# A DiT block on one core: reordering the transposes, scale matmuls and modulations of the first four chunks of the K projection

## The chip, the cores and the metric

The kernel runs on one core of one Trainium2 chip. The metric is device time in microseconds (us), median over executions. A profile is the trace of a single execution; its span (first to last instruction) is about 1.8 us shorter than the device time of the same execution. The kernels ran in four series, each with runs of before in it, and times are compared within a series: the second of the table of results ran on chip 3, the third on chip 9, another with experiments alone on chip 15. A load "lands" when all its data have arrived. Engines are named TensorE (PE), VectorE (DVE), ScalarE (ACT), GpSimd (POOL). "PEld" is TensorE's weight load.

## The reference

```python
mod = (_silu(c) @ w_mod).reshape(B, 6, 1, D)          # B, N, D = 2, 256, 1152
shift_a, scale_a, gate_a, shift_m, scale_m, gate_m = [mod[:, i] for i in range(6)]
h = _layernorm(x) * (1 + scale_a) + shift_a
qkv = (h @ wqkv)...                                    # then attention, wo, residual
... h2 = _layernorm(x) * (1 + scale_m) + shift_m; m = _gelu(h2 @ w_fc1) @ w_fc2
```

Only the beginning matters: normalise x, multiply by (1 + scale_a), multiply by the K part of wqkv. The kernel adds the shift later.

## The kernel before

x has 512 rows: four tiles of 128 (tiles 0 and 1 are batch 0, tiles 2 and 3 are batch 1). D = 1152 is nine chunks of 128. To feed TensorE, each tile is normalised by VectorE (`norm1`, which needs the tile's `rstd`, the reciprocal of its standard deviation), transposed chunk by chunk on TensorE into PSUM (`transpose_x`; PSUM is the memory that the kernel's matmuls and transposes write to, in parts called banks), and multiplied by the scale while it is copied out of PSUM (`modulate`). The scales themselves come from TensorE (`scale_group`) and from weights that are still being loaded. `k_step(k, ...)` does the K matmuls of chunk k for six of the nine output panels of 128 columns; the other three ("wide panels", L311 in the traces) follow when all chunks are done. The parts that the change touches:

```python
def scale_group(k0, k1, tile_of=aux_tile):
    pm = tile_of([P, k1 - k0, B], "pm")
    for j in range(k0, k1):
        ...                                   # 9 matmuls with 2 columns for each chunk j
            nc.tensor.matmul(pm[:, j - k0, :], w_scale_a[:, k, j * P:(j + 1) * P], sT[:, k, 0:B], ...)
def modulate(pt, i, k, b, j0, eng):
    dst, src, sc = hT0[:, k, b * N:(b + 1) * N], pt[:, i, j0:j0 + N], scale_a[:, k, b:b + 1]
    ...                                       # VectorE if eng == "d", else ScalarE
def both(pt, k):
    for b, e in enumerate("da"):
        modulate(pt, 0, k, b, b * N, e)
...
norm1(1, 0, CUT); norm1(0, 0, CUT)            # CUT = 4 chunks = 512 columns
pt_a = transpose_x([0, 1], BT[0])             # chunks 0-1 of tiles 0 and 1
... root_exp(2, 3)                            # ScalarE: rstd of tile 2, the last one
norm1(3, 0, CUT)
pm0, pm1 = [scale_group(k, k + 1, acc_tile) for k in range(2)]
nc.vector.tensor_scalar_mul(hT0[:, 0, 0:N], pt_a[:, 0, :], pm0[:, 0, 0:1])
... modulate(pt_a, 1, 1, 0, 0, "d")
norm1(2, 0, CUT)
transpose_x([0, 1], [3], pt_c, 1)
fill(1)                                       # one filler matmul of 512 columns
k_step(0, 0, N); k_step(1, 0, N, 0, 2)        # batch 0
transpose_x([0, 1], [2], pt_c, 0)             # needs tile 2's norm
k_step(1, 0, N, 2)
modulate(pt_c, 0, 0, 1, 0, "d"); modulate(pt_c, 1, 1, 1, 0, "a")
...
k_step(0, N, T)                               # batch 1
pm = scale_group(2, 4)
pt_b = transpose_x([2, 3], BT[0])
... k_step(1, N, T)
pt_d = transpose_x([2, 3], BT[1])
... k_step(2, 0, N); k_step(2, N, T)
for k in range(3, KD):
    split = 2 if k == 5 else 0
    k_step(k, 0, T, 0, split)
    if k in (3, 5, 7): scale_add(scale_group(k + 1, k1), ...)
    if k < KD - 1: both(transpose_x([k + 1], range(NT)), k + 1)
    k_step(k, 0, T, split)
```

## Time and profile before

| | us |
|---|---|
| device time before the prediction, median of 3 runs | 243.68 (243.38 to 243.81) |
| span of the profiled execution (its device time: 243.17) | 241.4 |
| TensorE busy | 236.6 (98%) |
| K projection: first transpose to first wide panel matmul (start 8.48, end 25.38) | 16.89 |

From the page of before: busy time of the engines, then the chain of work that ended last, by engine.

```profile
PE 236.6 (98%) x1698; PEld 144.9 (60%) x1698; DVE 91.5 (38%) x193; ACT 59.9 (25%) x121; POOL 28.3 (12%) x47
...
PE 94%; issue 2%; ACT 2%; POOL 1%; DVE 0%; POOLq 0%; DVEq 0%; ACTq 0%
```

TensorE bounds the kernel. A change at the start can only shorten the time by removing TensorE's breaks there. The timeline of TensorE in before, 8.4 to 14 us (columns: start us, us, engine, line, operation, output<-inputs, shapes, count; consecutive instructions of one group are merged):

```profile
8.48 0.40 PE L266 MATMUL pt<-ident,xn 128*128 128x128 bf16 x4 [0.23 <-DVE xn L235]
8.81 0.17 PE L247 MATMUL pm<-ones_row 1*128 1x2 bf16 x1
8.91 0.60 PE L249 MATMUL pm<-sT,w_scale_a 128*128 128x2 bf16 x18
9.38 0.27 PE L266 MATMUL pt<-ident,xn 128*128 128x128 bf16 x2
9.49 0.38 PE L325 MATMUL pwarm<-zeros 128*128 128x512 bf16 x1
9.74 1.03 PE L282 MATMUL pk<-big,w_k 128*128 128x256 bf16 x8
11.07 0.28 PE L266 MATMUL pt<-ident,xn 128*128 128x128 bf16 x2 [0.30 <-DVE xn L235]
11.19 1.42 PE L282 MATMUL pk<-big,w_k 128*128 128x256 bf16 x10
12.45 0.59 PE L249 MATMUL pm<-sT,w_scale_a 128*128 128x2 bf16 x18
12.91 0.38 PE L266 MATMUL pt<-ident,xn 128*128 128x128 bf16 x4
13.13 0.82 PE L282 MATMUL pk<-big,w_k 128*128 128x256 bf16 x6
13.78 0.39 PE L266 MATMUL pt<-ident,xn 128*128 128x128 bf16 x4
```

How to read it: the second column runs to the end of the last matmul's result, which lies some 0.2 us behind its issue; so count starts, not ends. Unmerged, a K matmul of 256 columns starts every 0.109 us and a transpose every 0.056 us. A bracket gives the engine's idle time before the instruction and what ended it; for TensorE it counts from the end of the last result, and is so some 0.16 us less than what the stream of issues lost. Eight K matmuls from 9.74 on are issued by 10.61, yet the next transposes start at 11.07: 0.46 us of waiting. Inside the ten matmuls from 11.19 on, the fifth starts 0.28 us after the fourth instead of 0.11: a second wait of 0.17. What they wait for, from the timelines of ScalarE and VectorE in before:

```profile
10.31 0.20 ACT L340 ACTIVATE rstd<-rstd 128x1 f32<-128x1 f32 x1
...
10.60 0.41 DVE L235 TENSOR_SCALAR xn<-x_sb,mv,rstd 128x512 bf16<-128x512 bf16 x1 [0.40 <-ACT rstd L340]
11.40 0.35 DVE L272 TENSOR_SCALAR big<-pt,scale_a 128x256 bf16<-128x256 bf16 x1 [0.38 <-PE pt L266]
```

ScalarE's rstd of tile 2 ends at 10.51, VectorE's norm of tile 2 runs 10.60 to 11.01, the transposes follow, then VectorE's modulation of chunk 0, batch 1, until 11.75. That chain (rstd, norm, transpose, modulation, matmul) is the critical path of this stretch.

### The profile page before, as it was taken

The page shows a single profiled execution, that of the slowest core. Times are in us where ns is not written, and L with a number is a line of the kernel's source. Part 1 is how long each engine was busy: PE and PEld are TensorE (multiplying, and loading weights), DVE is VectorE, ACT ScalarE, POOL GpSimd, SP SyncE. Part 2 cuts the span into 40 slices and gives each one's busy share as a digit, 9 for nine tenths or more (in the row PEclk, how much of TensorE's full clock was granted, in tenths as well). Part 3 has the DMA queues.
Part 4 walks back from the last instruction along what each step waited for, and adds up shares of the span by engine and source line. Part 5 has one row for each costly group of instructions (what it writes and reads, how often), then busy time and mean ns, then how long its engine had stood idle before and what let it go on. Part 6 is the DMA issues. An engine that isn't in the chain of part 4 may idle for free.

```text
span 241.4 us, 3989 instructions
## 1 busy us (share of the span) xinstructions
PE 236.6 (98%) x1698; PEld 144.9 (60%) x1698; DVE 91.5 (38%) x193; ACT 59.9 (25%) x121; POOL 28.3 (12%) x47
## 2 busy tenths in 40 slices
PE   8999999999999999999999999999999999999994
PEld 5675444476667666888844444444666666566674
DVE  4842442319325678830002999950000000000001
ACT  6723322307215032771423333222000000000000
POOL 2300000002300324100000000001121111111111
PEclk9999999999999999999999999999999999999999
DMA  6999999996599997739999999999200000000000
GB/s 221 323 316 322 376 368 393 388 392 214 120 332 397 388 272 77 196 61 366 390 391 391 339 326 282 278 327 281 98 16 16 20 16 16 19 18 17 26 25 16
DMA packets 48925, 53.30 MB, mean 221 GB/s; under 512 B 9731, under 2 KB 36619, under 8 KB 48907
## 3 DMA queue, kind: packets, MB, share of 16 engines
q1 hardware_dynamic: 41312, 50.14, 62.4%
q10 hardware_dynamic: 7083, 1.72, 5.3%
q0 software_dynamic: 512, 1.19, 1.8%
q8 instruction: 13, 0.21, 0.4%
q14 instruction: 5, 0.04, 0.1%
HBM read 50.15 MB, written 1.19 MB: 213 GB/s over the span
## 4 chain that ended last, share of the span: by engine, by line
PE 94%; issue 2%; ACT 2%; POOL 1%; DVE 0%; POOLq 0%; DVEq 0%; ACTq 0%
PE pacc L748 29%; PE pacc L804 29%; PE pacc L695 7%; PE pacc L601 7%; PE pq L523 7%; PE pk L282 5%; PE pk L311 2%; PE pa L642 2%; PE ps_s L558 2%; PE pn L418 2%; ACT sink L208 1%; PE pt L266 1%; PE pm L249 1%; PE pg L500 0%; ACT rstd L337 0%
## 5 line engine op out<-in xcount | busy, mean ns | idle before, releaser
L748 PE MATMUL pacc<-hT,w_f 128*128 128x256 bf16 (+1 forms) x432 | 70.5, 326 | 0.0
L804 PE MATMUL pacc<-w_f,gT 128*128 128x384 bf16 (+2 forms) x468 | 70.5, 314 | 0.0
L804 PEld LDWEIGHTS <-gT 128*128 128x128 bf16 x468 | 44.4, 98 | 26.2
L748 PEld LDWEIGHTS <-w_f 128*128 128x128 bf16 x432 | 42.2, 98 | 27.6
L810 DVE TENSOR_TENSOR tmp<-pacc,gate 128x384 f32<-128x384 f32 (+2 forms) x13 | 6.9, 527 | 65.6 <-PE pacc L804 57.4
L780 ACT ACTIVATE gT<-pacc 128x512 bf16<-128x512 f32 x24 | 14.3, 597 | 32.7 <-PE pacc L748 32.7
L471 DVE SCALAR_TENSOR_TENSOR part<-w_gate_m,s,part 128x1152 f32<-128x1152 bf16 x16 | 21.3, 1409 | 0.0
L812 POOL TENSOR_TENSOR o_sb<-tmp,x 128x384 bf16<-128x384 f32 (+1 forms) x12 | 11.7, 972 | 54.0 <-DVE tmp L810 54.0
L695 PE MATMUL pacc<-w_o,big 128*128 128x384 bf16 x108 | 17.9, 326 | 0.0
L523 PE MATMUL pq<-hT,w_q 128*128 128x512 bf16 x81 | 17.8, 379 | 0.0
L601 PE MATMUL pacc<-w_v,hT 128*128 128x384 bf16 x108 | 17.7, 326 | 0.0
L601 PEld LDWEIGHTS <-hT 128*128 128x128 bf16 x108 | 10.5, 98 | 7.1 <-issue 0.3
L695 PEld LDWEIGHTS <-big 128*128 128x128 bf16 x108 | 10.4, 98 | 7.2 <-issue 0.4
L523 PEld LDWEIGHTS <-w_q 128*128 128x128 bf16 x81 | 7.9, 98 | 9.4
L282 PE MATMUL pk<-big,w_k 128*128 128x256 bf16 (+1 forms) x72 | 13.3, 326 | 0.0
L701 POOL TENSOR_TENSOR x<-tmp,x_sb 128x384 f32<-128x384 f32 x8 | 7.3, 912 | 26.8 <-DMA w_scale_m<-in_w_mod_dram 14.9
L469 DVE TENSOR_SCALAR part<-w_gate_m,s 128x1152 f32<-128x1152 bf16 x2 | 1.5, 816 | 22.1 <-DMA w_gate_m<-in_w_mod_dram 22.1
L493 POOL DMA_DIRECT2D gates_dram<-nat_v x2 | 1.1, 534 | 67.7 <-DVE nat_v L491 67.7
L282 PEld LDWEIGHTS <-w_k 128*128 128x128 bf16 x72 | 6.7, 98 | 3.7 <-issue 0.3
L769 ACT ACTIVATE gT<-pacc 128x512 bf16<-128x512 f32 x12 | 6.5, 598 | 8.8 <-PE pacc L748 8.8
L514 POOL DMA_DIRECT2D gates_dram<-nat x4 | 2.4, 602 | 49.6 <-DVE nat L511 48.7
L175 PE MATMUL pwarm<-zeros 128*128 128x256 f32 x18 | 7.0, 560 | 1.2 <-DVE eps_t L95 1.2
(102 smaller groups left out, 164.9 us busy)
## 6 DMA issues: line engine op xcount, KB each, us to landing
w_f<-in_w_fc_dram SPq DMA_DIRECT2D x12, 864.0 KB, 14.3
w_f<-in_w_fc_dram SPq DMA_DIRECT2D x3, 1728.0 KB, 10.0
w_f<-in_w_fc_dram SPq DMA_DIRECT2D x2, 2592.0 KB, 17.3
w_gate_a<-in_w_mod_dram SPq DMA_DIRECT2D x3, 864.0 KB, 12.7
w_v<-in_wqkv_dram SPq DMA_DIRECT2D x3, 864.0 KB, 13.9
w_o<-in_wo_dram SPq DMA_DIRECT2D x3, 864.0 KB, 14.0
w_shift_m<-in_w_mod_dram SPq DMA_DIRECT2D x3, 864.0 KB, 8.8
w_scale_m<-in_w_mod_dram SPq DMA_DIRECT2D x3, 864.0 KB, 15.0
```

Source lines behind the costliest of these rows:

```text
L175: nc.tensor.matmul(dst[:, 0:T // 2], zeros32[:, 0:P], zeros32, start=True, stop=True)
L282: nc.tensor.matmul(pk[m][:, c0:c1], w_k[:, k, m * P:(m + 1) * P], hT0[:, k, c0:c1], start=(k == 0 and c0 == 0), stop=(k == KD - 1), skip_g ...
L471: nc.vector.scalar_tensor_tensor(part[:, b, :], wg[:, k, :], s32[:, k, b:b + 1], part[:, b, :], op0=ALU.mult, op1=ALU.add,)
L523: nc.tensor.matmul(pq[m][:], w_q[:, k, m * P:(m + 1) * P], hT[:, k, :], start=(k == 0), stop=(k == KD - 1), skip_group_check=True,)
L601: nc.tensor.matmul(pacc[:], hT[:, k, t * P:(t + 1) * P], w_v[:, k, pnl * PW:(pnl + 1) * PW], start=(k == 0), stop=(k == KD - 1),)
L695: nc.tensor.matmul(pacc[:], aT[:, k, t * P:(t + 1) * P], w_o[:, k, c0:c1], start=(k == 0), stop=(k == KD - 1),)
L701: (nc.gpsimd if pool_add else nc.vector).tensor_tensor(x1[:, t, c0:c1], tmp[:], x_sb[:, t, c0:c1], op=ALU.add)
L748: nc.tensor.matmul(dst, w_f1[m // KD][:, k, ml * P:(ml + 1) * P], hT[:, k, c0:c1], start=start, stop=(k == KD - 1), **kw,)
L780: nc.scalar.activation(gT[:, m, :], pacc[:], ACT.Gelu_apprx_tanh)
L804: nc.tensor.matmul(pacc[:], gT[:, kk, t * P:(t + 1) * P], w_f2[j][:, r, c0 - n * PW:c0 - n * PW + cw], start=(kk == 0), stop=(kk == KF - 1),)
L810: nc.vector.tensor_tensor(tmp[:], pacc[:], gate_m[:, b, c0:c0 + cw], op=ALU.mult)
L812: (nc.vector if last else nc.gpsimd).tensor_tensor(o_sb[:], tmp[:], x1[:, t, c0:c0 + cw], op=ALU.add)
```

## The change

Its intent: transpose all four chunks of tiles 0 and 1 at once, and of tile 3 too, before tile 2 is ready; put the scales of chunks 2-3 into the part of the same bank that is no longer used; let ScalarE and VectorE share modulations; and split tile 2's norm so that its first two chunks can be transposed earlier.

```diff
-    pt_a = transpose_x([0, 1], BT[0])
+    pt_a = transpose_x([0, 1, 2, 3], BT[0])
...
-    norm1(2, 0, CUT)
-    pt_c = aux_tile([P, 2, N], "pt", BF16)
-    transpose_x([0, 1], [3], pt_c, 1)
+    norm1(2, 0, N)
+    norm1(2, N, CUT)
+    pt_c = aux_tile([P, 4, N], "pt", BF16)
+    transpose_x([0, 1, 2, 3], [3], pt_c, 1)
     fill(1)                                   # and the filler has 256 columns instead of 512
     k_step(0, 0, N)
     k_step(1, 0, N, 0, 2)
+    modulate(pt_c, 0, 0, 1, 0, "a", P, N)
     transpose_x([0, 1], [2], pt_c, 0)
     k_step(1, 0, N, 2)
-    modulate(pt_c, 0, 0, 1, 0, "d")
+    modulate(pt_c, 0, 0, 1, 0, "d", 0, P)
...
     k_step(0, N, T)
-    pm = scale_group(2, 4)
-    pt_b = transpose_x([2, 3], BT[0])
+    pm = pt_a[:, 0, 0:4 * B].bitcast(FP32).rearrange("p (j b) -> p j b", b=B)
+    scale_group(2, 4, pm=pm)
+    for i in (2, 3):
+        nc.tensor.transpose(pt_c[:, i, 0:P], xns[2][:, i * P:(i + 1) * P], ident[:])
     scale_add(pm, 2, 4)
-    modulate(pt_b, 0, 2, 0, 0, "d")
-    modulate(pt_b, 1, 3, 0, 0, "a")
+    for b, e in enumerate("da"):
+        for i in (2, 3):
+            modulate((pt_a, pt_c)[b], i, i, b, 0, e)
     norm1(2, CUT, D)
+    norm1(3, CUT, D)
     k_step(1, N, T)
-    pt_d = transpose_x([2, 3], BT[1])         # and the modulations and the norm that followed it
     k_step(2, 0, N)
     k_step(2, N, T)
     for k in range(3, KD):
-        split = 2 if k == 5 else 0
+        split = 2 if k in (3, 5) else 0
```

More of the change, by code (lines that the diff above doesn't have):

```diff
@@ L241, with scale_group @@
     scale_a = act.tile([P, KD, B], FP32, name="scale_a")
-    def scale_group(k0, k1, tile_of=aux_tile):
-        pm = tile_of([P, k1 - k0, B], "pm")
+    def scale_group(k0, k1, tile_of=aux_tile, pm=None):
+        if pm is None:
+            pm = tile_of([P, k1 - k0, B], "pm")
         for j in range(k0, k1):
@@ L267, in transpose_x, with modulate @@
         return pt
-    def modulate(pt, i, k, b, j0, eng):
-        dst, src, sc = hT0[:, k, b * N:(b + 1) * N], pt[:, i, j0:j0 + N], scale_a[:, k, b:b + 1]
+    def modulate(pt, i, k, b, j0, eng, c0=0, c1=N):
+        dst, src, sc = hT0[:, k, b * N + c0:b * N + c1], pt[:, i, j0 + c0:j0 + c1], scale_a[:, k, b:b + 1]
         if eng == "d":
-            nc.vector.tensor_scalar_mul(dst, src, sc)
-        else:
-            nc.scalar.mul(dst, src, sc)
+            return nc.vector.tensor_scalar_mul(dst, src, sc)
+        return nc.scalar.mul(dst, src, sc)
     pk = [None] * KD
@@ L324, in fill @@
         for _ in range(n):
-            nc.tensor.matmul(pwarm[:], zeros[:, 0:P], zeros[:], start=True, stop=True)
+            nc.tensor.matmul(pwarm[:, 0:N], zeros[:, 0:P], zeros[:, 0:N], start=True, stop=True)
     def pool_eps(t):
@@ L384 @@
     k_step(0, N, T)
-    pm = scale_group(2, 4)
-    pt_b = transpose_x([2, 3], BT[0])
+    pm = pt_a[:, 0, 0:4 * B].bitcast(FP32).rearrange("p (j b) -> p j b", b=B)
+    scale_group(2, 4, pm=pm)
+    for i in (2, 3):
+        nc.tensor.transpose(pt_c[:, i, 0:P], xns[2][:, i * P:(i + 1) * P], ident[:])
     scale_add(pm, 2, 4)
-    modulate(pt_b, 0, 2, 0, 0, "d")
-    modulate(pt_b, 1, 3, 0, 0, "a")
+    for b, e in enumerate("da"):
+        for i in (2, 3):
+            modulate((pt_a, pt_c)[b], i, i, b, 0, e)
     norm1(2, CUT, D)
+    norm1(3, CUT, D)
     k_step(1, N, T)
-    pt_d = transpose_x([2, 3], BT[1])
-    modulate(pt_d, 0, 2, 1, 0, "d")
-    modulate(pt_d, 1, 3, 1, 0, "a")
-    norm1(3, CUT, D)
     k_step(2, 0, N)
```

## The prediction

> **What bounds the kernel now.** TensorE. The page gives PE busy 236.6 us of a 241.4 us span (98%), and the granted clock is 1.0 in all slices. The chain of waits is 94% PE. The change touches only the K projection's start, 8.5 to 25.4 us; there the timeline of PE, start to start, is nearly packed. The only breaks I find are:
> - 10.61 to 11.07: 0.46 us, waiting for tile 2's norm (DVE, 512 columns, 0.41 us, itself started at 10.60 when ScalarE's rstd came at 10.51);
> - 11.63 to 11.80: 0.17 us, waiting for the modulation of chunk 0, batch 1 (DVE, 256 columns, 0.35 us);
> - the filler matmul at 9.49: 0.22 us, then 0.04 us for the modulation of chunk 0;
> - 0.05 us before chunk 6 at 21.04.
>
> So at most about 0.9 us is there to win.
>
> **What the change does, step by step** (estimates from the durations in the trace)
> 1. Transposes: 16 for chunks 0-3 before and after, 56 ns each, so no PE work goes. But 4 now stand ahead of the first scale group: that group, the first modulation and the first K matmul slip 0.22 us, to about 9.96. The filler halves (0.11 us less) and is hidden.
> 2. K matmuls end at 10.84 instead of 10.61. Tile 2's norm still starts at 10.60, because rstd sets it. Its first half has 256 columns; 512 cost 0.41 and 640 0.44, so 256 should cost about 0.34: the split wins only 0.07. PE resumes at about 11.00 (before 11.07). The slip is swallowed by this wait, which shrinks from 0.46 to about 0.17.
> 3. The half modulation on DVE costs about 0.22 instead of 0.35, so the second wait shrinks from 0.17 to about 0.04. ScalarE's half (about 0.37, from 10.54) ends near 10.91, just before the transposes need the bank. The Trainium skill, "PSUM — Partial Sum Buffer", section "PSUM bank collisions raise a hardware error", says that engines must be kept apart per bank; the trace agrees: ScalarE's modulation starts 34 to 38 ns after VectorE's of the same bank ends. So this half could delay the transposes by some hundredths.
> 4. Scale 2-3 starts at about 12.25 (before 12.45). Six second-half matmuls (0.65 us) must now cover the scale's add and chunk 2's modulation; before, 4 more transposes lay between. I expect a new wait of 0.08 us before chunk 2.
> 5. Chunk 3's split keeps scale 4-5 at about 15.30. Its weights landed at 14.75, so DMA does not stop it. Chunk 4's matmuls then start at about 17.1 (before 17.51), with perhaps 0.05 us of new wait for ScalarE's modulation.
>
> Net: about 0.4 us earlier from chunk 4 on. Transfers until w_v do not depend on it. Slack of landings before: K's last columns 0.7 us, w_shift_a 0.6 us, so 0.4 us fits, narrowly. Later PE is packed and no wait on DMA bounds it (waits view: PE idles on nothing large), so the gain should survive to the end.
>
> **Predicted time**: 243.68 - 0.4 = 243.3 us; 242.8 to 243.8 holds it 8 times in 10. Faster by over 2%: 0.01; within 2%: 0.97; slower by over 2%: 0.02.
>
> **What would show it right or wrong** (timeline): first K matmul near 9.96; the wait for tile 2's norm near 0.17 and PE resuming near 11.0; a gap under 0.1 before batch 1's chunk 0; chunk 2 near 13.55; chunk 4 near 17.1; the first matmul of the wide panels near 24.97 instead of 25.38; span near 241.0.
>
> **What would make it wrong**: bank ordering that chains ScalarE's half, transposes and VectorE's half one after another; chunk 3's two modulations on ScalarE coming late; the weights of K's last columns or w_shift_a landing after PE, which would cap the gain near 0.6; noise of 0.2 us, half the effect.

## The result, and the profile after

| runs taken together | before, median | after, median | ratio after/before, 95% interval |
|---|---|---|---|
| first | 243.59 (6 runs) | 243.07 (6 runs) | 0.9984 (0.9971 to 0.9996) |
| second | 243.42 (11 runs) | 243.32 (6 runs) | 0.9995 (0.9980 to 1.0010) |
| third | 243.50 (9 runs) | 243.29 (5 runs) | 0.9993 (0.9981 to 1.0006) |

A ratio is the mean time of one kernel's runs over that of the other's of the same rounds, so it is not quite the ratio of the medians. The three ratios stand for gains of 0.39, 0.12 and 0.17 us, each with about 0.3 us to either side; the second and the third interval include no gain at all. The 0.52 us between the first medians is more than any trace below gives the change.

The first profile of after has a span of 241.3 us, only 0.13 less than before's. Its TensorE timeline, same window and columns:

```profile
8.64 0.62 PE L267 MATMUL pt<-ident,xn 128*128 128x128 bf16 x8 [0.70 <-DVE xn L235]
9.20 0.17 PE L248 MATMUL pm<-ones_row 1*128 1x2 bf16 x1
9.30 0.60 PE L250 MATMUL pm<-sT,w_scale_a 128*128 128x2 bf16 x18
9.77 0.38 PE L267 MATMUL pt<-ident,xn 128*128 128x128 bf16 x4
9.99 0.27 PE L325 MATMUL pwarm<-zeros 128*128 128x256 bf16 x1
10.13 1.03 PE L282 MATMUL pk<-big,w_k 128*128 128x256 bf16 x8
11.08 0.29 PE L267 MATMUL pt<-ident,xn 128*128 128x128 bf16 x2
11.21 1.43 PE L282 MATMUL pk<-big,w_k 128*128 128x256 bf16 x10
12.47 0.59 PE L250 MATMUL pt<-sT,w_scale_a 128*128 128x2 bf16 x18
12.92 0.27 PE L390 MATMUL pt<-ident,xn 128*128 128x128 bf16 x2
13.03 1.37 PE L282 MATMUL pk<-big,w_k 128*128 128x256 bf16 x11
```

Read it against before's: eight transposes instead of four stand at the head, four instead of two behind the first scales, and only two instead of eight behind 12.47. The work was moved ahead of 11.08, where TensorE had been waiting: eight K matmuls from 10.13 are issued by 11.00, so the wait for tile 2 is now 0.09 us. But the profile began 0.16 us later (8.64 against 8.48), so little shows yet at 11.08. ScalarE and VectorE in after:

```profile
10.38 0.20 ACT L340 ACTIVATE rstd<-rstd 128x1 f32<-128x1 f32 x1
10.49 0.35 ACT L274 ACTIVATE big<-pt,scale_a 128x128 bf16<-128x128 bf16 x1
...
10.68 0.60 DVE L235 TENSOR_SCALAR xn<-x_sb,mv,rstd 128x256 bf16<-128x256 bf16 x2
11.48 0.28 DVE L273 TENSOR_SCALAR big<-pt,scale_a 128x128 bf16<-128x128 bf16 x1 [0.20 <-PE pt L267]
```

And the list of waits of the weight loads of after between 8 and 26 us has a line that before's lacks (who waited for whom, us in total, times, longest):

```profile
PEld L250 <- DMA w_scale_a<-in_w_mod_dram: 0.7, 2, 0.5
```

The total is the weight load's idle time and overlaps matmuls still running. TensorE itself lost 0.12 us there: scale group 6-7's first matmul was issued at 19.10, where its place in the stream was 18.97, because its weights landed at 19.05 (17.81 in before's profile):

```profile
19.10 0.60 PE L250 MATMUL pm<-sT,w_scale_a 128*128 128x2 bf16 x18
```

**From 24 us on, the starts of all TensorE instructions keep the same distance in both, and in all fourteen profiles of this case, to within 0.003 us.** From the first wide panel matmul (L311) to the end of the span, before takes 216.015 us and after 216.016 us. So in the profiled executions nothing is gained or lost later on TensorE, and whatever moves the start of that matmul moves the time. Before and after, from the timelines of TensorE:

```profile
25.38 0.81 PE L311 MATMUL pk<-big,w_k 128*128 128x512 bf16 x3
```

```profile
25.25 1.03 PE L311 MATMUL pk<-big,w_k 128*128 128x512 bf16 x4
```

### The profile page after: what moved, and what is told of

It is laid out like the page before. It is cut to its first block, busy times and chain, and to the rows that moved or that the text cites. A ratio compares the mean times of both kernels' runs of the same rounds, so it can differ in the third digit from the quotient of the medians.

```text
span 241.3 us, 3993 instructions
## 1 busy us (share of the span) xinstructions
PE 236.3 (98%) x1698; PEld 144.6 (60%) x1698; DVE 91.6 (38%) x194; ACT 60.1 (25%) x122; POOL 28.3 (12%) x47
## 4 chain that ended last, share of the span: by engine, by line
PE 95%; DMA 2%; DVE 1%; SPq 0%; issue 0%; DVEq 0%
PE pacc L806 29%; PE pacc L750 29%; PE pacc L697 7%; PE pacc L603 7%; PE pq L525 7%; PE pk L282 5%; PE pk L311 2%; DMA x_sb<-in_x_dram 2%; PE pa L644 2%; PE ps_s L560 2%; PE pn L420 2%; PE pt L267 1%; PE pm L250 1%; DVE stats L195 1%; PE pg L502 0%; SPq L88 0%
```

## The experiments

Two theories compete. **A:** the order of TensorE's work in the K projection is worth a fixed few tenths of a us. **B:** what was measured is only where the loads happen to land, which differs from execution to execution. Inside A there is a second question: which part of the change is worth something?

The table gathers every profile, in us. "rstd" is the end of ScalarE's rstd of tile 2, "panel" the first wide panel matmul, "late weights" what TensorE lost to weights of the K projection that landed late after tile 2's norm. The last column is panel minus rstd minus late weights. (Weights of scale 0-1 were late in some profiles too, by up to 0.6 us; that fell into the wait for tile 2 and cost nothing.)

| kernel | tile 2 landed | rstd | panel | late weights | rest |
|---|---|---|---|---|---|
| before | 6.47 | 10.51 | 25.38 | 0 | 14.87 |
| before again | 6.89 | 10.54 | 25.43 | 0.02 | 14.87 |
| before, scale weights not awaited | 7.37 | 10.76 | 25.62 | 0 | 14.86 |
| before, no late loads | 6.98 (not awaited) | 10.53 | 25.39 | 0 | 14.86 |
| after | 7.21 | 10.59 | 25.25 | 0.12 | 14.54 |
| after again | 6.91 | 10.47 | 24.99 | 0 | 14.52 |
| after, third | 7.62 | 10.99 | 25.52 | 0 | 14.52 |
| after, scale weights not awaited | 7.47 | 10.85 | 25.38 | 0 | 14.53 |
| after, no late loads | 6.59 (not awaited) | 10.52 | 25.05 | 0 | 14.53 |
| after, VectorE whole | 6.85 | 10.61 | 25.75 | 0.62 | 14.53 |
| after, norm whole | 7.84 | 11.22 | 26.05 | 0.23 | 14.60 |
| after, chunk 3 unsplit | 7.05 | 10.49 | 25.34 | 0.35 | 14.49 |
| after, other load order | 7.45 | 10.84 | 26.31 | 0.93 | 14.54 |
| after, VectorE both | 7.53 | 10.91 | 25.36 | 0 | 14.46 |

### Both kernels again

No edit.

> The kernel before, unchanged, for a second profile and more times. The one profile of before reads 241.4 us and belongs to an execution of 243.17 us, faster than all six timed ones (243.38 to 243.81), so I expect it to be a lucky one: here a profile nearer to 243.6, with the first transposes later than 8.48 us because the tiles of x land later. Theory A (TensorE's waits in the K projection set the difference, about 0.4 us): the stretch from the first transpose to the first wide panel matmul is again 16.89 us plus or minus 0.1 when no weight is late. Theory B (the measured 0.4 us is only the landing of the loads, which differs from run to run): this stretch varies by several tenths between two profiles of the same kernel.

> The kernel after, unchanged. Ratio near 0.998. Stretch from the first transpose to the first wide panel matmul: 16.60 us in the first profile, of which 0.12 was a wait for the weights of scale 6-7 that landed at 19.05 us. Theory A: 16.48 to 16.6, with or without that wait. Theory B: a spread as large as the difference of the two kernels.

Before again: 243.32 us (ratio to before itself 1.0000, interval 0.9988 to 1.0012, which is how well 6 runs can tell), stretch from first transpose to panel 16.92 us. After again: 243.32 us, single runs in two clusters (242.81, 242.87, 243.01 and 243.63, 243.73, 243.73), stretch 16.50 us, span 241.0. The stretch was as theory A expects: 16.89 and 16.92 for before, 16.60 (16.48 without the late weights) and 16.50 for after. The new profile of before belongs to an execution of 243.26 us, not near 243.6 as expected. The profile of after again is the fastest execution of its six; its panel line:

```profile
24.99 1.24 PE L311 MATMUL pk<-big,w_k 128*128 128x512 bf16 x5
```

But the times are not: the ratio, 0.9995, has an interval that includes 1. So A holds in the traces, and B has a part in the times.

### After, with VectorE modulating chunk 0 whole

```diff
-    modulate(pt_c, 0, 0, 1, 0, "a", P, N)
...
-    modulate(pt_c, 0, 0, 1, 0, "d", 0, P)
+    modulate(pt_c, 0, 0, 1, 0, "d")
```

> After, with chunk 0 of batch 1 modulated by VectorE in one piece of 256 columns and ScalarE's half left out. Theory A: nothing lost. The half took 0.284 us and its instruction started 0.07 later, because it waited for two engines; the whole should take 0.35 and start without that, so the second-half matmuls of chunk 0 start 0.73 us after tile 2's transposes in both, and the time is the same within 0.05 us. Rival (the engines' sharing is where the gain comes from, as the change intends): 0.13 us later there and in the time.

Time 243.54 us (ratio 1.0005, 0.9993 to 1.0017); the time expectation can't be judged from it, since 0.62 us of this profile is a late load. The trace decides. VectorE and then TensorE in this kernel:

```profile
11.43 0.35 DVE L273 TENSOR_SCALAR big<-pt,scale_a 128x256 bf16<-128x256 bf16 x1
...
19.60 0.60 PE L250 MATMUL pm<-sT,w_scale_a 128*128 128x2 bf16 x18 [0.45 <-DMA w_scale_a<-in_w_mod_dram]
```

The second-half matmuls of chunk 0 start 0.729 us after tile 2's transposes; in after it was 0.734. **Sharing chunk 0 between the engines is worth nothing.** The half of 128 columns takes 0.284 us, the whole 0.352: 0.067 us saved. But the half starts 0.110 us after the transposes' end and the whole 0.038: the half waits for two engines (TensorE and ScalarE), and a separate wait instruction stands before it in the trace (the two halves share no data, so the shared bank is the likely reason for the second wait). The line's instructions in after, then in this kernel (DVEq is VectorE's sequencer; count, shortest/median/longest in ns, first and last start in us):

```profile
L273 DVEq EVENT_SEMAPHORE  x1: 21/21/21, 11.4 to 11.4; - x1
L273 DVE TENSOR_SCALAR big<-pt,scale_a x1: 284/284/284, 11.5 to 11.5; 128x128 bf16<-128x128 bf16 x1
...
L273 DVE TENSOR_SCALAR big<-pt,scale_a x1: 352/352/352, 11.4 to 11.4; 128x256 bf16<-128x256 bf16 x1
```

0.07 saved, 0.07 paid. The Trainium skill, "Perfetto Trace Analysis", section "Identifying Dependency Chains", says that instructions which wait for several engines may get such extra wait instructions; this trace agrees and puts a price on it.

### After, with tile 2's norm whole

```diff
-    norm1(2, 0, N)
-    norm1(2, N, CUT)
+    norm1(2, 0, CUT)
```

> After, with tile 2's norm in one piece of 512 columns. Theory A: the norm takes 0.41 instead of 0.35 us, so tile 2's transposes start 0.07 us later after ScalarE's rstd (0.56 instead of 0.50 us after its end), and the stretch from first transpose to first panel grows by 0.07 us to 16.55 plus any wait for weights. Rival (the split is worth half of the norm, 0.2 us): 0.2 us.

Time 243.63 us (ratio 1.0003, 0.9988 to 1.0017; runs from 242.88 to 243.92, so the times tell nothing of 0.07). The trace: rstd ended at 11.22, the norm and then the transposes that wait for it were

```profile
11.31 0.41 DVE L235 TENSOR_SCALAR xn<-x_sb,mv,rstd 128x512 bf16<-128x512 bf16 x1 [0.18 <-ACT rstd L340]
...
11.78 0.28 PE L267 MATMUL pt<-ident,xn 128*128 128x128 bf16 x2
```

so the transposes came 0.562 us after rstd, against 0.497 in after; and the last column of the table is 14.60 against 14.52 to 14.54. The split is worth 0.07 us, as expected.

### Both kernels without a wait for scale weights

The scale matmuls read the identity matrix; the loads are still issued. The result is wrong.

```diff
-    pm[:, j - k0, :], w_scale_a[:, k, j * P:(j + 1) * P], sT[:, k, 0:B],
+    pm[:, j - k0, :], ident[:], sT[:, k, 0:B],
```

> The kernel before, whose scale matmuls read the identity in place of the scale weights (a wrong result on purpose; the loads are still issued, nothing waits for them). Theory A': the change is worth 0.40 us of TensorE's order in the K projection, but late scale weights (groups 0-1 and 6-7, which land up to 1.2 us apart from profile to profile) take part of it back, since an earlier kernel waits longer for the same landing. Then here: stretch from first transpose to first panel 16.9 us, no wait for scale weights, time 0 to 0.15 us under before. Rival (the gain is luck of the landings): nothing told apart from the pair below, both move by the same amount and differ by nothing.

> The kernel after with the same edit, wrong on purpose too. Theory A': stretch 16.50 us, no wait for scale weights, and the whole 0.4 us shows in the times: 0.35 to 0.5 us under the same edit of before, where the unedited pair differed by 0.1 to 0.5 from session to session. Rival: the two edited kernels run alike within 0.1 us.

Before with the edit 243.31 us (5 runs, 243.21 to 243.72), after with it 243.44 us (6 runs, 242.89 to 245.59). Both expectations for the times failed. The unedited kernel before had a median of 243.80 us in the same series of runs (on chip 15), so the edit took 0.49 us off it (ratio 0.9982, 0.9967 to 0.9996) where 0 to 0.15 was expected; no unedited kernel was profiled in that series, so what it lost stays open. And the second kernel was not faster than the first: three of its executions took 243.71, 244.33 and 245.59 us (the last at a granted clock of 0.993). The profile taken belongs to one of the other three (243.18 us), so what lengthened those stays open too. The traces agree with theory A: 14.86 and 14.53. They show a second source of spread as well: here tile 2 of x landed at 7.37 and 7.47 us and rstd came late for it, at 10.76 and 10.85. In the seven profiles where tile 2 landed after 7.2 us and its statistics waited for it, rstd ended 3.37 to 3.39 us after the landing.

### After, with another order of loads

```diff
-        for a, z in [(0, 1), (1, 2)] if k0 == 0 else [(k0, k1)]:
+        for a, z in {0: [(0, 1), (1, 2)], 4: [(4, 5)], 6: [(5, 6), (6, 8)]}.get(k0, [(k0, k1)]):
```

> After, with the weights of chunk 5 of K loaded behind the scale weights of chunks 6-7 instead of ahead of them (the pair 4-5 is split; the result stays right). Theory A': these scale weights land about 0.6 us earlier (17.4 to 18.6), ahead of TensorE's need at 18.9; chunk 5's weights land near 18.2 to 19, needed at 18.4, so a short wait may come there instead. If that one stays under 0.1 us, the time falls to 0.3 to 0.5 us under before, and no slow cluster is left. Rival (lateness of any load shifts to the next): the wait moves to chunk 5 and the time equals after's.

The rival was right, and more: 244.17 us (ratio 1.0014, 0.9998 to 1.0029). The scale weights of 6-7 landed at 18.09, in time, but chunk 5's K weights landed at 19.68 instead of 18.2 to 19, and TensorE waited 0.93 us for them:

```profile
19.72 0.60 PE L282 MATMUL pk<-big,w_k 128*128 128x512 bf16 x2 [0.77 <-DMA w_k<-in_wqkv_dram]
```

The span grew by another 0.4 us after TensorE's last matmul (3.52 us instead of 3.10). In this run, moving one load forward moved another back, behind TensorE's need.

### After, with chunk 3 unsplit

```diff
-        split = 2 if k in (3, 5) else 0
+        split = 2 if k == 5 else 0
```

> After, with chunk 3's matmuls unsplit, so the scale matmuls of chunks 4-5 come two matmuls (0.43 us) earlier, near 14.9 us. Theory A: no wait for ScalarE's modulation before chunk 4 (0.05 us less), but the scale weights of 4-5 landed at 14.75 to 15.95 in the profiles so far, so TensorE waits there up to 0.5 us in most runs; where it does, that wait is repaid only if it would have waited for the later scale weights too. Time: as after or up to 0.3 us longer. Rival (the split gains time by itself): 0.2 us or more longer with no wait for weights.

Time 243.45 us, 4 runs (ratio 0.9996, 0.9974 to 1.0017). In the trace, scale group 4-5 was ready at 14.91 us and waited for its weights (landed 15.22):

```profile
15.27 0.60 PE L250 MATMUL pm<-sT,w_scale_a 128*128 128x2 bf16 x18 [0.19 <-DMA w_scale_a<-in_w_mod_dram]
```

That lost 0.35 us, where after, with the split, lost 0.05 us to ScalarE's modulation. So the split of chunk 3 gains nothing in itself; here it puts the scale group behind the landing of its weights, as I expected. In this execution the wait also saved no later wait, because scale weights 6-7 landed early (18.22).

### Both kernels without late loads

To see the order of the work by itself in the times: no scale weights are loaded (the matmuls read the identity), and the statistics of tiles 2 and 3 are taken of tiles 0 and 1, which land first. Wrong results; the same instructions on the engines.

```diff
-        nc.sync.dma_start(w_scale_a[...], wmod_v[...])
-    pm[:, j - k0, :], w_scale_a[:, k, j * P:(j + 1) * P], sT[:, k, 0:B],
+    pm[:, j - k0, :], ident[:], sT[:, k, 0:B],
-    sink[:], x_sb[:, t, :], f, bias=x_sb[:, t, 0:1], scale=-1.0,
+    sink[:], x_sb[:, 0, :], f, bias=x_sb[:, 0, 0:1], scale=-1.0,
-    nc.vector.bn_stats(stats1[t][:, j, :], x_sb[:, t, j * PW:(j + 1) * PW])
+    nc.vector.bn_stats(stats1[t][:, j, :], x_sb[:, 1, j * PW:(j + 1) * PW])
```

> Before, with what differs from run to run at the start taken away (a wrong result on purpose): the scale weights are not loaded at all (their matmuls read the identity), and the statistics of tiles 2 and 3 are taken of tiles 0 and 1, so that they wait for no late load. Same instructions on every engine otherwise. In the eight profiles so far, the first wide panel matmul comes 14.86 to 14.89 us after ScalarE's rstd of tile 2 in before, and 14.53 in after once waits for scale weights are taken off. Theory A'' (the change is worth that 0.34 us; the landings of tile 2 and of scale 6-7 blur it): rstd near 10.5, first panel near 25.37, no wait for weights, times within 0.3 us of one another.

> After with the same edits, wrong on purpose too. Theory A'': first panel near 25.03, 14.53 us after rstd; 0.3 to 0.4 us faster than the same edit of before in the times too, with the two sets of times hardly overlapping. Rival (the gain in the K projection is given back later, or is luck): less than 0.15 us apart.

Before with the edit: 243.48, 243.49, 243.49, 243.61, 243.88; after with it: 243.07, 243.15, 243.16, 243.21, 243.36. The two sets do not overlap; the means are 243.59 and 243.19, 0.40 us apart (an estimate from the spread of these ten runs: 0.2 to either side), the medians 0.33. (Before's five runs lie 0.40 us apart, where 0.3 was expected.) rstd and panel of before, then of after (other line numbers, since lines were taken out):

```profile
10.32 0.20 ACT L336 ACTIVATE rstd<-rstd 128x1 f32<-128x1 f32 x1
...
25.39 0.81 PE L307 MATMUL pk<-big,w_k 128*128 128x512 bf16 x3
```

```profile
10.32 0.20 ACT L336 ACTIVATE rstd<-rstd 128x1 f32<-128x1 f32 x1
...
25.05 1.24 PE L307 MATMUL pk<-big,w_k 128*128 128x512 bf16 x5
```

rstd is the same to 0.001 us (10.525 and 10.524), the panel 0.338 us earlier. (Both spans end 0.3 us later behind TensorE's last matmul than the unedited kernels' do, in the same way in both.) This is the clean measure of the change: **0.34 us** in the trace, and times that agree with it within their spread, once the loads are out of the way.

### After once more, and a version that may beat both

The last kernel leaves out ScalarE's half, lets VectorE modulate both batches of chunks 4 to 8, and puts the scale groups behind three matmuls instead of two:

```diff
-        for b, e in enumerate("da"):           # in both()
+        for b, e in enumerate("dd"):
...
-    modulate(pt_c, 0, 0, 1, 0, "a", P, N)
-    modulate(pt_c, 0, 0, 1, 0, "d", 0, P)
+    modulate(pt_c, 0, 0, 1, 0, "d")
...
-        split = 2 if k in (3, 5) else 0
+        split = 3 if k in (3, 5) else 0
```

> After once more, beside the next kernel. Theory A'': first panel 14.53 us after rstd, plus what TensorE waits for scale weights of 6-7 if they land later than 8.34 us after rstd; time 0 to 0.4 us under before.

> A version that may beat both (result right): after, with ScalarE's half of chunk 0 left out, both batches of chunks 4-8 modulated by VectorE (second modulation 0.27 us after the first, instead of ScalarE's 0.47 behind it), and the scale groups of 4-5 and 6-7 one matmul (0.22 us) later behind three matmuls. Theory A'': the waits of 0.05 before chunks 4 and 6 fall to about 0.03 or less, so the first panel comes about 14.47 us after rstd; scale weights 6-7 may land 0.2 us later without a wait, so late landings cost less. Time 0.05 to 0.25 us under after's. Rival: VectorE's queue becomes the limit and chunk 4 starts later than 6.66 us after rstd.

After, third: 243.29 us (0.9993 of before, 0.9981 to 1.0006). The new version: 243.16 us (0.9985, 0.9973 to 0.9998), its mean 0.20 us under after's in the same series (243.08 against 243.28), 5 runs each. The trace gives it 0.07 us: 14.46 against 14.52. VectorE's two modulations, and ScalarE's rstd and the panel:

```profile
16.87 0.61 DVE L273 TENSOR_SCALAR big<-pt,scale_a 128x256 bf16<-128x256 bf16 x2
```

```profile
10.70 0.20 ACT L340 ACTIVATE rstd<-rstd 128x1 f32<-128x1 f32 x1
...
25.36 0.81 PE L311 MATMUL pk<-big,w_k 128*128 128x512 bf16 x3
```

Two modulations on VectorE take 0.61 us; VectorE's 0.35 and ScalarE's 0.47 behind it took 0.86. The waits before chunks 4 and 6 fell from 0.05 to 0.02 us each, which is that 0.07. Scale 6-7 is now needed 8.56 us after rstd instead of 8.38, so it may land later without harm; in this profile it landed in time and the benefit was not tried. The version is the fastest of its series with a right result (after's first median, 243.07, is lower still), but at 0.07 us in the trace and an interval that holds after's ratio, no more than that should be claimed.

## Why the prediction was right or wrong

The time was right: 243.3 us predicted, 243.07, 243.32 and 243.29 measured. The chance given to "within 2%" was right too. But the time is a weak test: the stated range, 242.8 to 243.8, holds before's own 243.68. The mechanism was right in its main step, and the sum of 0.4 us is 0.34 in the traces, because two terms were mis-sized.

The timeline's mark for the wide panels was missed once, and met once with some luck. They were to start at 24.97; they started at 25.25 in the first profile of after and at 24.99 in the second. In the first, rstd came 0.08 us later than in before's profile, late weights took 0.12, and some 0.06 is the mis-sized sum; in the second, rstd came 0.04 us earlier than in before's profile and hid most of that 0.06.

Counted from the end of rstd, in the traces of before and after:

- **Moving transposes into the wait (steps 1 and 2): right.** Six transposes went from behind tile 2's norm to before it: 6 x 0.056 = 0.33 us. The 0.22 us of slip at the head was swallowed, as predicted: first K matmul predicted 9.96, measured 9.96 in the second profile of after (10.13 in the first, whose transposes began 0.16 later); the wait for tile 2 predicted 0.17, measured 0.09 to 0.14 in after's three profiles, 0.17 without late loads (and 0.42 without a wait for scale weights, where tile 2 landed late and only it). No run moved the transposes alone; the 0.33 is counted from TensorE's timeline.
- **Splitting the norm (step 2): right.** 0.34 us predicted for the half, 0.346 measured; 0.07 us gained.
- **Halving the modulation of chunk 0 (step 3): wrong.** "About 0.22 instead of 0.35, so the second wait shrinks from 0.17 to about 0.04": it stayed at 0.17 to 0.18. The prediction took 0.13 us off for 128 columns, about 1.0 ns each; the half saved only 0.067 us, 0.52 ns each, so some 0.22 us of its 0.284 does not depend on the columns. The Trainium skill, "VectorE: DVE Perf Modes", section "Why PSUM operands drop a tier", allows a 16-bit PSUM operand the 2x_1P mode, two results per cycle, and its section "Specifications" gives a clock of 0.96 GHz; an estimate from the two is 0.52 ns per column, the measured 0.52 ns agrees with it, and I should have used it. And I left out the 0.07 us that a wait for two engines cost here. (ScalarE's modulations in before's K projection start 34 to 35 ns after VectorE's, not 34 to 38 as the prediction says.) The worry named in the prediction, that bank ordering could delay the transposes, did not come true: ScalarE's half ended at 10.84 and the transposes waited for the norm, which ended at 11.03.
- **The new wait before chunk 2 (step 4): mis-sized the other way.** 0.08 predicted, 0.015 measured. The modulation followed the scale's add after 0.035 us, not 0.107 as in before: here it waits for VectorE's own add alone, in before for TensorE's transposes too, with a separate wait instruction like the one above.
- **Chunk 3's split (step 5): right.** Scale 4-5 was not stopped by its weights; 0.05 us predicted for the wait before chunk 4, 0.05 measured. Without the split it is stopped (0.35 us).
- The sum, 0.33 + 0.07 - 0.015 - 0.05, is 0.34 when rounded up (0.335). The prediction's 0.40 was 0.33 + 0.07 + 0.13 - 0.08 - 0.05.
- **"The gain should survive to the end": right for the work behind 25 us,** which takes the same time to 0.001 us, **but not in every execution.** I checked the slack of K's last columns and of w_shift_a, and neither ever delayed TensorE. I did not check scale weights 6-7, which TensorE now wants 0.34 us sooner (8.38 instead of 8.73 us after rstd). In three of the five profiles that await these weights in after's order of loads and with its split, they landed after that and took back 0.12, 0.62 and 0.23 us. An estimate from those numbers: in the case of 0.62, before would have reached that group at 10.61 + 8.73 = 19.33 us and also have waited until 19.60, so there the change would have gained nothing.

So both theories have a share. The change is worth 0.34 us by the order of the work (shown by the pair without late loads). In the real kernels rstd of tile 2 came between 10.47 and 11.22 us, in seven profiles set by the landing of tile 2; that spread is larger than the gain, and late scale weights take a part of the gain away (shown in single traces). In both kernels all loads ahead of w_v are issued in the same order and on waits for earlier loads alone, so I take their landings for chance. That is not shown: tile 2 landed at 6.93 us on average in before's four profiles and at 7.25 in the ten of after and its variants, which is too few to tell from chance. Why they land at such different times, and what lengthened three runs of after without a wait for scale weights, stays open, and so does the exact mean gain of the unedited kernels: three estimates of 0.1 to 0.4 us, of which one interval alone excludes zero, are all that the times tell.

## What to carry to other kernels

Moving work that is ready into a wait that something else sets gained its full length here (0.33 us), where it fitted into the wait; shortening the instructions behind the wait gained only what was left after fixed costs (0.07 us for half of a norm of 0.41, or of a modulation of 0.35), and a shared instruction that had to wait for two engines cost what it saved. When a change makes one stage a few tenths faster, list every load that this stage needs with its landing time and its new deadline, not only the last ones: the gain holds only in executions where each lands before it. For effects smaller than the spread of the times, anchor the trace at the event that varies (here the rstd of the last tile) and compare distances from it; and take away the variable part in both kernels to confirm it in the times.

## What the Trainium skill lacked or had wrong

- "PSUM — Partial Sum Buffer", section "PSUM bank collisions raise a hardware error": says that engines must be kept apart per bank, not what the ordering costs. Here modulations that wait for one engine on the bank started 0.034 to 0.039 us after that engine's end (TensorE's ends are modelled by the profile); the half that waits for two started 0.110 us after the later one.
- "Perfetto Trace Analysis", section "Identifying Dependency Chains": names the extra wait instruction for several engines, without its cost. Here it was 0.07 us (0.110 against 0.038 us from transposes' end to modulation).
- "TensorEngine Tiling (Array Packing)", section "Key Properties": says that a change of tiling mode drains TensorE, without a number. Here TensorE lost 0.10 us before the single matmul with one row, between the transposes and the scale matmuls, in every profile, and 0.08 us behind it where no weights were late. That such a drain is the reason was not tested.
- No page that I read tells how far the landing of the same load can vary. Here tile 2 of x landed between 6.47 and 7.84 us, and scale weights 6-7 between 17.81 and 19.85 us, with the same loads issued in the same order.
